# Another split of the rows over the partitions in a fused attention and mixer kernel: four rows of a head on 64 partitions, three on the other 64

## The chip, the cores and the metric

One core of a Trainium2 chip runs the whole program. The time is device microseconds (us) of one execution, as the median of several; lower is better. Ratios below are the mean time of one kernel's fast runs over that of the other's fast runs of the same rounds, so not quite the ratio of the medians that are quoted. A run counts as slow when it is over 1.5% above the fastest of its kernel.

## The reference, cut to what matters

Cosine attention over 8 batches, 12 heads, 448 rows and 64 columns a head, then a mixer with a token part and a channel part. Everything comes in and goes out as 32-bit floats.

```
q_n = q / (norm(q) + 1e-6);  k_n = k / (norm(k) + 1e-6)
attn = softmax(q_n @ k_n.T / tau)
x   = (attn @ v) as [8, 448, 768]
h   = relu(x.T @ w_tok1) @ w_tok2         # 448 -> 256 -> 448
u   = x + h.T
out = u + relu(u @ w_ch1) @ w_ch2         # 768 -> 1536 -> 768
```

## The kernel before

The difficulty is the 448 rows: three and a half times 128 partitions. The kernel keeps 384 rows of a head as three rows on each of 128 partitions (the main loads, pieces of 768 B) and the last 64 rows apart, as one row on each of 64 partitions (pieces of 256 B). Heads are taken in pairs (48 in all), pairs in half batches of three.

```
P, NC, XR = 128, 3, 64;  SM = P * NC                       # 384 main rows, 64 more
def main(at, src, nm, n, g0=0, g1=6, bufs=3):
    ...
    return dict(out=at[n][:, g0:g1].rearrange("p g c e -> p g (c e)"),
                in_=half(src, n)[g0:g1, 0:SM].rearrange("g (p c) e -> p g (c e)", c=NC))
def load_q(n, g0=0, g1=6):
    nc.sync.dma_start(**main(qm, q, "qm", n, g0, g1))        # k and v alike
def load_xq(b, g0=0, g1=12):
    ...
    nc.sync.dma_start(out=xq[b][:, g0:g1], in_=q[b, g0:g1, SM:S].rearrange("g p e -> p g e"))
def load_x2(...):                                            # xk, xv: two heads on two halves
    for g in range(2):
        eng.dma_start(out=at[b][XR * g:XR * (g + 1), g0 // 2:g1 // 2], in_=r[g])
def weights_tok():                                           # GpSimd issues
    nc.gpsimd.dma_start(out=w1t[:, 0:NC, :], ...)
    nc.gpsimd.dma_start(out=w1t[0:XR, NC, :], ...)
    nc.gpsimd.dma_start(out=w2n[0][:], ...)                  # the second token weight
def place_w2():                                              # three copies put it in order
    nc.vector.tensor_copy(out=w2t[:, :, XR:S]..., in_=w2n[0][:, :, 0:SM]...)
    for lo in (0, S):
        nc.vector.tensor_copy(out=w2t[:, :, lo:lo + XR], in_=w2n[0][:, :, SM:S])
...
# a store of an output row block
nc.sync.dma_start(out=out[b, 0:SM].rearrange("(p c) d -> c p d", c=NC)[m][:, cols], in_=o[:, cols])
```

Nearly all loads, all stores and the transposes by DMA (of u throughout, of q, k and x from pair 15 on) are issued by one engine, SyncE, in program order: "the queue" below. GpSimd issues the weights and scales and squares q and k; TensorE does all products.

Of the kernel before, what the change touches and what calls it, by code (L numbers as in the profile page):

```python
# [22 lines left out]
def kernel(  # L23
# [18 lines left out]

    P = 128
# [3 lines left out]
    E1 = E + 1  # L47
    DT = D // P
# [16 lines left out]
    qkv = ctx.enter_context(tc.tile_pool(name="qkv", bufs=3))  # L65
# [14 lines left out]
    sqx = cst.tile([P, 9, E], FP32, name="sqx")  # L80
    ssqs = [cst.tile([P, 45], FP32, name=f"ssq{i}") for i in range(3)]
    rns = [cst.tile([P, 45], FP32, name=f"rn{i}") for i in range(3)]
    kqs = [cst.tile([P, HP, 2, NC + 1, 2 * E], FP16, name=f"kq{i}") for i in range(2)]
    vts = [cst.tile([P, 6, NC, E + 2], FP16, name=f"vt{i}") for i in range(NV)]
    vxs = [cst.tile([P, HP, 2 * E1 + 2], FP16, name=f"vx{i}") for i in range(NV)]
# [3 lines left out]
    qm, km, vm, xq, xk, xv = {}, {}, {}, {}, {}, {}  # L89
# [4 lines left out]
    def half(src, n):  # L94
        return src[n // 2, 6 * (n % 2):6 * (n % 2) + 6]



    def main(at, src, nm, n, g0=0, g1=6, bufs=3):
        if n not in at:  # L100
            at[n] = qkv.tile([P, 6, NC, E], FP32, name=f"{nm}_{n}", tag=nm, bufs=bufs)
        return dict(out=at[n][:, g0:g1].rearrange("p g c e -> p g (c e)"),
                    in_=half(src, n)[g0:g1, 0:SM].rearrange("g (p c) e -> p g (c e)", c=NC))

    def load_q(n, g0=0, g1=6):
        nc.sync.dma_start(**main(qm, q, "qm", n, g0, g1))

    def load_k(n, g0=0, g1=6, eng=nc.sync):
        eng.dma_start(**main(km, k, "km", n, g0, g1))

    def load_v(n):
        nc.sync.dma_start(**main(vm, v, "vm", n, bufs=2))

    def load_xq(b, g0=0, g1=12):
        if b not in xq:
            xq[b] = qkv.tile([XR, H, E], FP32, name=f"xq_{b}", tag="xq", bufs=2)
        nc.sync.dma_start(out=xq[b][:, g0:g1], in_=q[b, g0:g1, SM:S].rearrange("g p e -> p g e"))

    def load_x2(at, src, nm, b, g0=0, g1=12, eng=nc.sync):
        if b not in at:  # L120
            at[b] = qkv.tile([P, NPAIR, E], FP32, name=f"{nm}_{b}", tag=nm, bufs=2)
        r = src[b, g0:g1, SM:S].rearrange("(j g) p e -> g p j e", g=2)
        for g in range(2):
            eng.dma_start(out=at[b][XR * g:XR * (g + 1), g0 // 2:g1 // 2], in_=r[g])  # L124

    def load_xk(b, g0=0, g1=12, eng=nc.sync):
        load_x2(xk, k, "xk", b, g0, g1, eng)

    def load_xv(b, g0=0, g1=12):
        load_x2(xv, v, "xv", b, g0, g1)  # L130



    def xh(at, n, w):
        return at[n // 2][:, w * (n % 2):w * (n % 2) + w]

    def mh(at, p):
        return at[p // HP][:, 2 * (p % HP):2 * (p % HP) + 2]

    def weights_tok():  # L140
        nc.gpsimd.dma_start(out=w1t[:, 0:NC, :], in_=moe_w_tok1[0:SM].rearrange("(p c) t -> p c t", c=NC))
        nc.gpsimd.dma_start(out=w1t[0:XR, NC, :], in_=moe_w_tok1[SM:S])
        w2n.append(mix.tile([P, TT, S], FP16, name="w2n", tag="gt16", bufs=1))
        nc.gpsimd.dma_start(out=w2n[0][:], in_=moe_w_tok2.rearrange("(tt p) s -> p tt s", p=P))

    def place_w2():
        nc.vector.tensor_copy(out=w2t[:, :, XR:S].rearrange("t a (c p) -> t a c p", c=NC),
                              in_=w2n[0][:, :, 0:SM].rearrange("t a (p c) -> t a c p", c=NC))
        for lo in (0, S):
            nc.vector.tensor_copy(out=w2t[:, :, lo:lo + XR], in_=w2n[0][:, :, SM:S])  # L150
# [12 lines left out]
    def cast_v(n):  # L163
        (nc.vector if n < 3 else nc.gpsimd).tensor_copy(out=vts[n % NV][:, :, :, 0:E].rearrange("p g c e -> p (g c) e"),
                              in_=vm[n][:].rearrange("p g c e -> p (g c) e"))
        for g in range(2):
            r = slice(XR * g, XR * (g + 1))
            nc.gpsimd.tensor_copy(out=vxs[n % NV][r, :, E1 * g:E1 * g + E], in_=xh(xv, n, HP)[r])

# [8 lines left out]
    def squares(p, eq, ek):  # L178
        sq[p] = nrm.tile([P, 2, 2 * NC, E], FP32, name=f"sq_{p}", tag="sq")
        for a, (eng, src) in enumerate(((eq, mh(qm, p)), (ek, mh(km, p)))):  # L180
            square(eng, sq[p][:, a], src.rearrange("p g c e -> p (g c) e"))

    def squares_x(n, eq, ek):
        square(eq, sqx[0:XR, 0:6], xh(xq, n, 6))
        square(ek, sqx[:, 6:9], xh(xk, n, HP))

    def sums(p, a0=0, a1=2):
        lo = 9 + 12 * (p % HP)
        nc.vector.tensor_reduce(out=ssqs[p // HP % 3][:, lo + 6 * a0:lo + 6 * a1],  # L189
                                in_=sq[p][:, a0:a1].rearrange("p a g e -> p (a g) e"), axis=AXX.X, op=ALU.add)  # L190

    def sums_x(n):
        nc.vector.tensor_reduce(out=ssqs[n % 3][:, 0:9], in_=sqx[:], axis=AXX.X, op=ALU.add)

    def rnorms(n, c0=0, c1=45):
        ssq, rn = ssqs[n % 3][:, c0:c1], rns[n % 3][:, c0:c1]
        nc.scalar.activation(out=rn, in_=ssq, func=AF.Ln, bias=tiny[:])
        nc.scalar.activation(out=rn, in_=rn, func=AF.Exp, scale=0.5)
        nc.scalar.activation(out=rn, in_=rn, func=AF.Ln, bias=eps[:])
        nc.scalar.activation(out=rn, in_=rn, func=AF.Exp, scale=-1.0)  # L200

    def scaled(p, eng):
        n, j = p // HP, p % HP
        for a, src in enumerate((mh(km, p), mh(qm, p))):
            lo = 9 + 12 * j + 6 * (1 - a)
            rn = rns[n % 3][:, lo:lo + 6].rearrange("p (g c) -> p g c", g=2)
            eng.tensor_tensor(out=kqs[n % 2][:, j, a, 0:NC, :].rearrange("p c (g e) -> p g c e", g=2),  # L207
                              in0=src, in1=_bcast_free(rn, E), op=ALU.mult)

    def scaled_x(n, eng, j0=0, j1=HP):  # L210
        rn, kq = rns[n % 3], kqs[n % 2]
        gs = slice(2 * j0, 2 * j1)
        eng.tensor_tensor(out=kq[0:XR, j0:j1, 1, NC, :].rearrange("p j (g e) -> p j g e", g=2),
                          in0=xh(xq, n, 6)[:, gs].rearrange("p (j g) e -> p j g e", g=2),
                          in1=_bcast_free(rn[0:XR, gs].rearrange("p (j g) -> p j g", g=2), E), op=ALU.mult)
        for g in range(2):
            r = slice(XR * g, XR * (g + 1))
            eng.tensor_tensor(out=kq[r, j0:j1, 0, NC, E * g:E * g + E], in0=xh(xk, n, HP)[r, j0:j1],
                              in1=_bcast_free(rn[r, 6 + j0:6 + j1], E), op=ALU.mult)
# [17 lines left out]
    def tpose_main(p, pst, a):  # L237
        for c in range(NC):
            nc.tensor.transpose(pst[:, P * (4 * a + c):P * (4 * a + c + 1)], kqs[p // HP % 2][:, p % HP, a, c], id16[:])  # L239

    def tpose_x(p, pst):
        kq = kqs[p // HP % 2]
        nc.tensor.transpose(pst[:, P * NC:P * (NC + 1)], kq[:, p % HP, 0, NC], id16[:])
        nc.tensor.transpose(pst[:, P * 7:P * 7 + XR], kq[0:XR, p % HP, 1, NC], id16[0:XR, 0:XR])
# [4 lines left out]
    def tpose(p):  # L249
        pst = pst_tile(p)  # L250
        tpose_main(p, pst, 0)
        tpose_main(p, pst, 1)
        tpose_x(p, pst)
# [11 lines left out]



    def score_main0(c, fill=0):
        qk, pt = qks[0], pts[0]
        psS = ps2.tile([P, 2, 512], FP32, name=f"psS_0_{c}", tag="s")  # L270
        busy(psS[:, 0, :], fill)
        for g in range(2):
            r = slice(E * g, E * g + E)
            nc.tensor.matmul(psS[:, g, 0:SM], qk[r, P * c:P * (c + 1)], qk[r, 512:512 + SM], start=True, stop=True)
        nc.scalar.activation(out=pt[:, 2 * S * c:2 * S * (c + 1)].rearrange("p (g s) -> p g s", g=2)[:, :, 0:SM],
                             in_=psS[:, :, 0:SM], func=AF.Exp, scale=inv_tau)

    def score_rest0():
        qk, pt = qks[0], pts[0]
        psS = ps2.tile([P, 2, 512], FP32, name="psS_0_r", tag="s")  # L280
        for c in range(NC):
            for g in range(2):
                r = slice(E * g, E * g + E)
                nc.tensor.matmul(psS[:, g, XR * c:XR * (c + 1)], qk[r, P * c:P * (c + 1)],
                                 qk[r, 512 + SM:512 + S], start=True, stop=True)
        for g in range(2):
# [191 lines left out]
    def loads(i):  # L478
        for n in q_at.get(i, ()):
            load_q(n)  # L480
        for b in xq_at.get(i, ()):
            load_xq(b)
# [277 lines left out]
```

## Time and profile before

| | before |
|---|---|
| time, median of the first three runs | 395.24 us (394.54 to 395.39) |
| span of the profiled execution | 395.6 us |
| TensorE busy | 379.0 us, 96% |
| loads and stores issued by the queue | 129, beside 108 transposes |
| queue occupied, 120 to 320 us | 162 of 200 us |

The queue is occupied for the sum of the durations of its rows in the timeline (small gaps between the issues of one row count in), in which the wait of an issue for its data is included. The lines of the page, the stretches and the waits stand in the prediction and are read there.

### The profile page before, as it was taken

How to read it: one execution, taken by the hardware profiler on the slowest of the kernel's cores; microseconds unless marked ns; L12 is line 12 of the kernel's file. 1: busy time of each engine (PE TensorE's matmuls, PEld its weight loads, DVE VectorE, ACT ScalarE, POOL GpSimd, SP SyncE). 2: the span in 40 equal slices, each digit the busy share in tenths (PEclk: the TensorE clock that was granted, in tenths of full speed). 3: DMA queues.
4: the chain of work that ended last, by engine and by line, in shares of the span. 5: the costliest groups of instructions: out<-in, count | busy, mean ns of one | idle time of the engine just before them, and what ended most of it. 6: DMA issues, size and time to landing. Idle time of an engine off the chain costs nothing.

```text
span 395.6 us, 9085 instructions
## 1 busy us (share of the span) xinstructions
PE 379.0 (96%) x3658; PEld 229.0 (58%) x3658; DVE 193.4 (49%) x368; ACT 226.3 (57%) x411; POOL 209.6 (53%) x306
## 2 busy tenths in 40 slices
PE   7498999998999999999999999999999999999997
PEld 2155656665556565656556666556556565666554
DVE  5668677964534555445623654536524442333022
ACT  5788799943485547675576347573676436510410
POOL 4957677579549393949492856749470800000000
PEclk9779999999999999999999999999999999999999
DMA  8999999989968988899999989999974363013013
GB/s 214 251 245 268 229 206 198 192 205 222 219 131 167 218 195 200 190 190 223 202 186 196 194 214 214 189 186 193 226 105 107 91 152 69 16 35 112 16 40 119
DMA packets 137482, 67.51 MB, mean 171 GB/s; under 512 B 93216, under 2 KB 133984, under 8 KB 137440
## 3 DMA queue, kind: packets, MB, share of 16 engines
q1 hardware_dynamic: 133264, 61.36, 72.1%
q0 software_dynamic: 3632, 5.18, 7.4%
q8 instruction: 28, 0.46, 0.5%
q10 hardware_dynamic: 544, 0.39, 0.3%
q14 instruction: 14, 0.11, 0.1%
HBM read 43.38 MB, written 11.01 MB: 138 GB/s over the span
## 4 chain that ended last, share of the span: by engine, by line
PE 87%; ACT 4%; DMA 4%; DVE 2%; SPq 1%; issue 0%; ACTq 0%; DVEq 0%
PE psF L400 28%; PE psG L385 27%; PE psO L316 9%; PE psS L297 7%; PE psR L337 5%; PE psU L357 4%; PE psO L318 3%; ACT pt L298 2%; PE psX L304 2%; DMA xk<-in_k_dram 2%; DMA km<-in_k_dram 1%; DMA out_dram<-ost 1%; PE psU L362 1%; PE pst L239 1%; DVE ost L403 1%; SPq L124 1%
## 5 line engine op out<-in xcount | busy, mean ns | idle before, releaser
L298 ACT ACTIVATE pt<-psS 128x896 f16<-128x896 f32 x141 | 119.0, 920 | 66.7 <-PE psS L297 66.5
L385 PE MATMUL psG<-ut,wc1t 128*128 128x448 f16 x576 | 119.5, 353 | 0.2
L400 PE MATMUL psF<-wc2t,gt 128*128 128x384 f16 (+2 forms) x684 | 117.3, 323 | 1.2 <-DVE ost L403 1.2
L387 ACT ACTIVATE gt<-psG 128x448 f16<-128x448 f32 x96 | 51.1, 556 | 73.2 <-PE psG L385 73.2
L400 PEld LDWEIGHTS <-gt 128*128 128x128 f16 x684 | 64.5, 98 | 48.4 <-issue 8.1
L207 POOL TENSOR_TENSOR kq<-km,rn 128x384 f16<-128x384 f32 x47 | 39.5, 841 | 85.0 <-ACT rn L200 84.7
L385 PEld LDWEIGHTS <-wc1t 128*128 128x128 f16 x576 | 53.2, 98 | 52.4 <-issue 8.7
L403 DVE TENSOR_TENSOR ost<-psF,ur 128x384 f32<-128x384 f32 (+2 forms) x57 | 31.4, 550 | 90.0 <-PE psF L400 86.6
L316 PEld LDWEIGHTS <-pt 128*128 128x128 f16 x1152 | 50.8, 98 | 11.3 <-issue 5.2
L316 PE MATMUL psO<-vt,pt 128*128 128x65 f16 x1152 | 53.2, 195 | 3.4 <-ACT pt L298 3.0
L322 DVE RECIPROCAL rec<-psO 128x8 f32<-128x8 f32 x48 | 9.9, 207 | 81.5 <-PE psO L318 81.4
L189 DVE TENSOR_REDUCE ssq<-sq 128x12 f32<-128x768 f32 (+1 forms) x49 | 45.1, 928 | 6.8 <-ACT sq L174 4.9
L318 PE MATMUL psO<-vx,pt 128*128 128x130 f16 x192 | 42.1, 219 | 0.0
L176 POOL TENSOR_TENSOR sq<-km 128x384 f32<-128x384 f32 x42 | 34.6, 826 | 11.3 <-DMA km<-in_k_dram 11.1
L207 POOL TENSOR_TENSOR kq<-qm,rn 128x384 f16<-128x384 f32 x47 | 39.6, 843 | 0.0
L297 PE MATMUL psS<-qk 64*128 64x448 f16 x282 | 36.5, 362 | 1.2 <-ACT pt L305 0.6
L323 DVE TENSOR_TENSOR x<-psO,rec 128x512 f16<-128x512 f32 x48 | 33.2, 691 | 1.7
L337 PE MATMUL psR<-x,w1t 128*128 128x128 f16 x384 | 29.2, 219 | 0.0
L305 ACT ACTIVATE pt<-psX 128x448 f16<-128x448 f32 x48 | 27.0, 563 | 3.5 <-PE psX L304 2.5
L357 PE MATMUL psU<-w2t,r 128*128 128x448 f16 x96 | 25.9, 353 | 1.8 <-DVE w2t L150 1.4
L176 POOL TENSOR_TENSOR sq<-qm 128x384 f32<-128x384 f32 x30 | 24.8, 827 | 3.7 <-DVE ssq L189 2.1
L337 PEld LDWEIGHTS <-w1t 128*128 128x128 f16 x384 | 23.8, 97 | 2.0 <-issue 0.3
(75 smaller groups left out, 319.8 us busy)
## 6 DMA issues: line engine op xcount, KB each, us to landing
vm<-in_v_dram SPq DMA_DIRECT2D x16, 576.0 KB, 5.4
out_dram<-ost SPq DMA_DIRECT2D x23, 384.0 KB, 3.1
qm<-in_q_dram SPq DMA_DIRECT2D x15, 576.0 KB, 5.4
km<-in_k_dram SPq DMA_DIRECT2D x15, 576.0 KB, 5.6
wc1t<-in_moe_w_ch_dram POOLq DMA_DIRECT2D x2, 1152.0 KB, 13.4
wc2t<-in_moe_w_ch_dram POOLq DMA_DIRECT2D x2, 1152.0 KB, 13.0
out_dram<-ost SPq DMA_DIRECT2D x9, 192.0 KB, 2.9
xq<-in_q_dram SPq DMA_DIRECT2D x7, 192.0 KB, 6.0
```

The lines of the kernel that those rows point to most:

```text
L176: eng.tensor_tensor(out=out, in0=src, in1=src, op=ALU.mult)
L189: nc.vector.tensor_reduce(out=ssqs[p // HP % 3][:, lo + 6 * a0:lo + 6 * a1], in_=sq[p][:, a0:a1].rearrange("p a g e -> p (a g) e"), axis=A ...
L207: eng.tensor_tensor(out=kqs[n % 2][:, j, a, 0:NC, :].rearrange("p c (g e) -> p g c e", g=2), in0=src, in1=_bcast_free(rn, E), op=ALU.mult)
L297: nc.tensor.matmul(psS[:, g, 0:S], qk[r, P * c:P * (c + 1)], qk[r, 512:512 + S], start=True, stop=True)
L298: nc.scalar.activation(out=pt[:, 2 * S * c:2 * S * (c + 1)].rearrange("p (g s) -> p g s", g=2), in_=psS[:, :, 0:S], func=AF.Exp, scale=inv ...
L316: nc.tensor.matmul(psO[:, m, E1 * g:E1 * (g + 1)], pt[:, at:at + P], vt[:, 2 * j + g, c, 0:E1], start=(g == 0 and c == 0), stop=False)
L318: nc.tensor.matmul(psO[:, m, 0:2 * E1], pt[:, PX + P * m:PX + P * (m + 1)], vx[:, j, 0:2 * E1], start=False, stop=True)
L337: nc.tensor.matmul(psR[:, tt, :], w1t[:, m, tt * P:(tt + 1) * P], xs[p][:, m, :], start=(m == 0), stop=(m == NC))
L357: nc.tensor.matmul(psU, rs[p][:, tt, :], w2t[:, tt, lo:lo + S], start=(tt == 0), stop=by_dma and tt == TT - 1)
L385: nc.tensor.matmul(psG[:], wc1t[:, dt, ct * P:(ct + 1) * P], ut[:, dt, sp], start=(dt == 0), stop=(dt == DT - 1))
L387: nc.scalar.activation(out=gt[:, ct, sp], in_=psG[:], func=AF.Relu)
L400: nc.tensor.matmul(psF[:, 0:w], gt[:, ct, lo:lo + P], wc2t[:, ct, P * i0:P * i1], start=(ct == 0), stop=(ct == CT - 1))
```

## The change

Its intent: drop the small loads. On 64 partitions a head has four rows, on the other 64 three (4 x 64 + 3 x 64 = 448), so the last 64 rows come with the main ones in pieces of 1024 or 768 B, and norms, scalings and casts lose their extra instructions for the last rows. For every second head of k and v the halves are mirrored, so that the fourth rows of two heads fill 128 partitions. No load of q, k or v spans 128 partitions. The second token weight is issued later, and slots 0 to 6 (one slot per pair) are ordered by hand.

```
+    def parts(mirrored):
+        four, three = (0, XR * CH, CH), (XR * CH, S, NC)        # CH = 4
+        if mirrored:
+            four, three = (XR * NC, S, CH), (0, XR * NC, NC)
+        return ((three, four) if mirrored else (four, three))
     def load_q(n, j0=0, j1=HP):
-        nc.sync.dma_start(**main(qm, q, "qm", n, g0, g1))
+        for i, (lo, hi, c) in enumerate(parts(False)):
+            nc.sync.dma_start(out=qms[n % 3][XR * i:XR * (i + 1), 2 * j0:2 * j1, 0:c]..., in_=...)
     def load_k(n, j0=0, j1=HP):                                  # v alike
+        for g in range(2):
+            for i in range(2):
+                load_heads(kms[n % 3], k, n, g, i, j0, j1)       # 64 partitions, 3 heads
-    load_xq, load_x2, load_xk, load_xv, squares_x, sums_x, scaled_x, score_main0, score_rest0
...
-            nc.sync.dma_start(out=out[b, 0:SM]...[m][:, cols], in_=o[:, cols])
+            for i, (r0, r1, c) in enumerate(parts(False)):
+                nc.sync.dma_start(out=out[b, r0:r1]...[m][:, cols], in_=o[XR * i:XR * (i + 1), cols])
...
     q_at: the load of q for half batch 7 (counted from 0) from slot 12 to slot 13
     weights_tok2() (the second token weight): from behind weights_tok1() to the end of slot 1
     place_w2(): four copies instead of three
... (slots 0 to 6 spelled out)
```

## The prediction

> **What bounds the kernel now.** I read the page first, then the busy time by stretches, then the waits of TensorE, then the chain of waits, then the order in time of each engine from 0 to 50 us and near 90 us.
>
> From the page, the engines' busy time and the 40 slices:
>
> ```profile
> PE 379.0 (96%) x3658; PEld 229.0 (58%) x3658; DVE 193.4 (49%) x368; ACT 226.3 (57%) x411; POOL 209.6 (53%) x306
> ...
> PE   7498999998999999999999999999999999999997
> ...
> PEclk9779999999999999999999999999999999999999
> ```
>
> TensorE is busy 379.0 of 395.6 us, so 16.6 us is all that any better order of the same matmuls can win, plus what a reduced clock costs. The stretches say where:
>
> ```profile
> 0.00:10.00 10.00, 7.37 (x28) 2.77 (x28) 5.34 (x15) 5.84 (x16) 4.74 (x21) 1.00 0.85 214
> 10.00:20.00 10.00, 4.25 (x37) 1.95 (x37) 6.12 (x11) 8.02 (x20) 9.15 (x14) 0.77 1.06 253
> 20.00:30.00 10.00, 8.84 (x97) 5.43 (x95) 7.22 (x12) 8.80 (x19) 5.66 (x7) 0.72 0.99 243
> 30.00:40.00 10.00, 8.59 (x130) 6.15 (x130) 7.83 (x16) 8.36 (x16) 7.50 (x12) 1.00 1.10 267
> ...
> 90.00:100.00 10.00, 8.83 (x88) 5.59 (x86) 4.52 (x10) 3.08 (x4) 9.71 (x15) 1.00 1.04 248
> ...
> 160.00:200.00 40.00, 40.00 (x389) 23.77 (x387) 20.85 (x43) 23.80 (x41) 29.32 (x42) 1.00 1.03 202
> ```
>
> Columns: stretch, length, busy TensorE, weight load, VectorE, ScalarE, GpSimd, granted clock, DMA share, GB/s. TensorE's gaps are 2.6, 5.8, 1.2 and 1.4 us in the first four stretches, 1.2 us at 90 to 100, none from 110 to 380, and about 2.9 us at the very end, where only the last store runs. The clock is 0.77 and 0.72 from 10 to 30 us. Everything winnable is thus in the first 100 us. The waits of TensorE name what ended the gaps:
>
> ```profile
> PE psO L316 <- ACT pt L298: 3.0, 2, 2.8
> PE pst L243 <- DVE kq L218: 1.8, 1, 1.8
> PE psU L357 <- DVE w2t L150: 1.4, 1, 1.4
> PE busy L232 <- POOL id L536: 1.4, 1, 1.4
> PE psF L400 <- DVE ost L403: 1.2, 1, 1.2
> ```
>
> And the chain of waits near the start shows a load behind the largest one:
>
> ```profile
> 11.51 6.98 DMA xk<-in_k_dram
> 18.49 0.03 ACTq L174
> 18.52 0.04 issue
> 18.56 0.36 ACT sqx L174
> 18.92 0.81 ACT pt L298
> ```
>
> The small load of the last 64 rows of k is under way for 6.98 us; ScalarE, which works in order, stands before its square until 18.56, and only then makes the exponentials of pair 1, on which the first output matmul (19.78) waits.
>
> [...] The removed loads move 256 B pieces. [...] with the queue full, the slices between 13.5 and 15.5 us move 106 to 206 GB/s, while the first main loads move about 340 to 375. [...] The trace has no half-partition main load; an issue takes 0.5 to 0.6 us on the queue whatever its size. [...] the granted clock is 0.50 from about 15.3 to 25.7 us, after a stretch (10 to 14 us) with 1.2 us of matmuls in 4.
>
> **The change part by part.**
>
> *Loads.* Removed: 96 heads x 64 rows x 3 tensors = 18,432 pieces of 256 B of 137,482 packets. Queue 1's 133,264 packets took 72.1% of 16 x 395.6 us, 34 ns each, so this takes away about 39 us of each DMA engine's 395: up to a tenth of the DMA load. From 110 us on TensorE never waits, so this counts only at the start. Added: half a batch took 3 main issues and on average 2.5 small ones; it now takes 10 (q 2, k 4, v 4). Each out row block becomes 2 stores. In all 96 more issues, at about 0.57 us, 55 us more of the queue's time.
>
> *Wider elementwise work.* Squares and scalings go from 384 to 512 columns. On GpSimd 192 to 384 columns is 503 to 827 ns, so 512 is about 1,043 ns. Per half: before, 6 scalings at 0.84 plus extra rows 0.84 + 2 x 0.525 = 6.95, squares 6.28, casts 1.18 + 0.69: 15.1 us. After: 12 x about 1.05 plus a cast of about 1.55: 14.2 us. VectorE sums: 3 x 0.945 + 0.744 = 3.58 before; 3 x (0.945 + 0.264) = 3.63 after. Neither is on the path after 110 us.
>
> *TensorE.* The same columns; 6 tiny matmuls of pair 0 go. Nothing.
>
> *The start, followed by hand with before's durations.* Pair 0 comes as six loads; the last is issued near 1.8 us, so k is squared near 5.0 (before 4.50). The k loads of pairs 1 and 2 are issued [...]near 4.1 to 5.8, and land near 9.5. ScalarE squares k of pair 1 before it copies the transposes of pair 0, so the first score moves from 10.18 to about 10.6. From there it is better: the whole score runs at once (no second part with its 1.8 and 0.9 us waits), the score of pair 1 comes near 15.3 (before 15.71), the exponentials of pair 1 no longer stand behind the late small load: they start near 16.5 instead of 18.83, the first output matmul near 17.4 to 18 instead of 19.78, the score of pair 2 near 21 instead of 23.88. So up to 2.8 us is won by then.
>
> *Then part is given back.* The load of the second token weight moves from 14.6 us to behind pair 5's squares on GpSimd. Its chain: scale pair 2 to 16.8, square pairs 3 and 4 to 18.9, norms of pair 3 done near 20, scale pair 3 to 22, square pair 5 to 23. Issued at 23, at some 5 us to landing (6.9 before, in a fuller queue), it lands near 28; VectorE then needs 2 us to place it: first product with it near 30.2, against 30.54. The gain shrinks from 2.8 to about 0.3 us. In slot 5 the new order puts norms (1.0 us) between the exponentials and the last one of pair 5, where before they stood a slot earlier beside an idle ScalarE: about 0.8 us given back. I make the start worth between -1 and +2 us, about +0.3.
>
> *Near 90 us.* The 1.2 us wait is for a store: it left at 92.43 although its data were ready near 85.3, because the queue stood before q's load (issued 89.33), which waited for GpSimd to release its buffer. The change moves this load one slot later, behind the stores. I count +1.2 us.
>
> *The end.* The last store becomes two issues of half the rows: about -0.4 us.
>
> Sum of the central terms: 0.3 + 1.2 - 0.4 = about 1.1 us off, so 394.1. The slots were evidently set by hand to fit, which my rough timing of the second weight may undervalue; I move to 393.5.
>
> **The rivals.**
>
> *The second weight decides.* For: TensorE already waited 1.4 us for its placement, and it is now issued some 8 us later. If it lands at 30, the start loses 1.5 us: about 396. If at 26, VectorE is ready near 27 anyway and 1.5 to 2 us are won: about 391.5.
>
> *The whole start is won.* If the pieces of 256 B were the real brake, loads land far earlier, [...]the clock stays full (worth up to 2.3 us) and nearly all of the 9 us of gaps from 8 to 50 us go: 386 to 388. Against: ScalarE is busy 8.0 to 8.8 of 10 us there; it becomes the bound first.
>
> *The issuing queue becomes the bound.* From 160 to 200 us it is occupied 36.9 of 40 us. About 7 us more would fill it, transposes would come late, and TensorE would wait in the steady part: 398 to 405. Against: much of the 36.9 us is the wait for GpSimd and VectorE inside an issue (a transpose takes 1.2 us at least and up to 3.6), and these results come no later than before.
>
> **Range and chances.** Two per cent is 7.9 us of a ceiling of roughly 12 (8 to 110 us) plus 2.3 of clock; only the second rival reaches it: 0.04. Slower by 2% needs the third in earnest: 0.03. Within 2%: 0.93. The range 390 to 397 spans the first rival's both ends with the 90 us term in or out.
>
> **What would show each step right or wrong.** Of the changed kernel: exponentials of pair 1 starting near 16.5; first output matmul before 18.5; half clock ending before 25.7; the wait for the placed weight still among TensorE's waits, with its first product near 30; the wait for ost near 97 gone; no waits of TensorE from 110 to 380; the end's gap longer by some 0.4 us; fewer packets under 512 B by 18,432. Waits of TensorE in the steady part for qk or xT would mean the queue; a first product with the placed weight before 28 us or score of pair 4 before 32 would mean that I undervalue the start.

## The result, and the profile after

| | before | after |
|---|---|---|
| time, median of 4 runs each | 395.31 us (394.54 to 396.47) | 427.47 us (425.51 to 429.47) |
| ratio | | 1.0811 (95%: 1.0754 to 1.0868) |
| span, mean granted clock | 395.6 us, 0.987 | 427.7 us, 0.961 |
| TensorE busy | 379.0 us | 388.8 us |
| loads and stores issued by the queue | 129 | 223 |
| queue occupied, 120 to 320 us | 162 us | 187 of 200 us |

The change made the kernel 8% slower. First the stretches of the kernel after, with the columns of the prediction's table:

```profile
10.00:20.00 10.00, 7.26 (x59) 3.61 (x57) 5.81 (x7) 7.26 (x16) 4.57 (x5) 0.79 1.08 223
20.00:30.00 10.00, 7.23 (x66) 4.40 (x64) 7.05 (x10) 7.28 (x16) 6.34 (x7) 0.53 1.12 223
30.00:40.00 10.00, 4.06 (x34) 2.49 (x34) 3.82 (x8) 2.54 (x3) 6.37 (x7) 0.82 1.15 225
...
90.00:100.00 10.00, 3.53 (x20) 2.04 (x20) 0.69 (x2) 1.29 (x4) 3.73 (x4) 0.72 1.24 175
...
200.00:320.00 120.00, 112.84 (x1087) 67.43 (x1085) 54.62 (x102) 64.41 (x111) 68.95 (x67) 0.99 0.86 184
```

and the one stretch of before that the prediction did not show:

```profile
200.00:320.00 120.00, 120.00 (x1182) 72.51 (x1181) 55.70 (x110) 70.66 (x120) 71.92 (x101) 1.00 0.88 178
```

The 32.1 us between the spans are 9.8 us of longer busy time (388.8 - 379.0, the same columns at a lower clock: see 0.53 from 20 to 30 and 0.72 from 90 to 100) and 22.3 us of idling. By stretch (rounded), idle time after minus before: 3.7 us from 0 to 50, 8.6 from 50 to 100, 1.2 from 100 to 200, 7.2 from 200 to 320 and 1.8 at the end (4.7 us behind the last product in place of 2.9). So TensorE loses in every part, and also where before it never waited. What it waited for, after:

```profile
PE psF L350 <- DMA wc2t<-in_moe_w_ch_dram: 7.3, 1, 7.3
PE psU L307 <- DVE w2t L144: 5.9, 1, 5.9
PE psG L335 <- DVE ost L353: 5.4, 3, 2.2
...
PE psS L208 <- DVE x L273: 2.7, 1, 2.7
PE psS L247 <- DVE ut L317: 2.0, 3, 1.1
```

Each line: the tile TensorE was to write, what released it, us in total, times, longest. Of the lines shown, the first is the landing of the second channel weight near 96 us, the second the placed second token weight at 37.2, the third output tiles that had not been stored yet, the last the sum that needs a transposed x from the queue. The second and fourth are of the start, the third and fifth of 110 to 330 us. The queue of the kernel after, in a stretch of that part (start, duration, issue):

```profile
203.61 1.62 SPq L236 DMA_TRANSPOSE qk<-kq  x1
205.32 1.68 SPq L280 DMA_TRANSPOSE xT<-x  x1
207.09 1.22 SPq L326 DMA_TRANSPOSE ur<-ut  x1
208.37 2.57 SPq L114 DMA_DIRECT2D km<-in_k_dram  x4
211.03 1.19 SPq L362 DMA_DIRECT2D out_dram<-ost  x2
212.33 1.36 SPq L236 DMA_TRANSPOSE qk<-kq  x1
```

and of the kernel before, for the same kind of slot:

```profile
189.89 0.57 SPq L112 DMA_DIRECT2D vm<-in_v_dram  x1
190.51 1.30 SPq L124 DMA_DIRECT2D xv<-in_v_dram  x2
191.91 0.56 SPq L410 DMA_DIRECT2D out_dram<-ost  x1
192.57 1.50 SPq L261 DMA_TRANSPOSE qk<-kq  x1
```

Each issue starts where the one before it ends. A load of k takes 2.57 us of the queue where a main load of 128 partitions (of v, above) took 0.57, and a store 1.19 instead of 0.56. The bytes are the same (67.5 MB in both), and the packets fell from 137,482 to 120,506.

### The profile page after: what moved, and what is told of

Its sections match the earlier page's. It is cut to its first block, busy times and chain, and to the rows that moved or that the text cites. A ratio compares the mean times of both kernels' runs of the same rounds, so it can differ in the third digit from the quotient of the medians.

```text
span 427.7 us, 9048 instructions
## 1 busy us (share of the span) xinstructions
PE 388.8 (91%) x3652; PEld 233.7 (55%) x3652; DVE 197.0 (46%) x354; ACT 224.7 (53%) x397; POOL 195.8 (46%) x204
## 2 busy tenths in 40 slices
DMA packets 120506, 67.51 MB, mean 158 GB/s; under 512 B 76304, under 2 KB 116944, under 8 KB 120464
## 4 chain that ended last, share of the span: by engine, by line
PE 63%; DMA 14%; SPq 8%; POOL 6%; DVE 3%; ACT 3%; issue 2%; DVEq 0%; POOLq 0%; ACTq 0%
PE psG L335 21%; PE psF L350 20%; PE psO L266 6%; SPq L114 5%; PE psS L247 5%; DMA wc2t<-in_moe_w_ch_dram 5%; POOL kq L194 4%; PE psR L287 3%; PE psU L307 3%; DMA km<-in_k_dram 3%; DMA out_dram<-ost 3%; DMA w2n<-in_moe_w_tok_dram 2%; DMA xT<-x 2%; PE psO L268 2%; POOL sq L172 2%
## 5 line engine op out<-in xcount | busy, mean ns | idle before, releaser
L248 ACT ACTIVATE pt<-psS 128x896 f16<-128x896 f32 x144 | 122.0, 920 | 72.2 <-PE psS L247 72.2
L194 POOL TENSOR_TENSOR kq<-km,rn 128x512 f16<-128x512 f32 x46 | 47.9, 1042 | 79.8 <-ACT rn L189 75.7
L172 POOL TENSOR_TENSOR sq<-km 128x512 f32<-128x512 f32 x42 | 43.8, 1046 | 40.8 <-DMA km<-in_k_dram 40.8
L180 DVE TENSOR_REDUCE ssq<-sq 128x16 f32<-128x1024 f32 (+1 forms) x49 | 57.9, 1188 | 8.4 <-POOL sq L172 4.4
L266 PEld LDWEIGHTS <-pt 128*128 128x128 f16 x1152 | 52.7, 100 | 6.9 <-issue 0.4
L266 PE MATMUL psO<-vt,pt 128*128 128x65 f16 x1152 | 55.4, 197 | 0.2
L194 POOL TENSOR_TENSOR kq<-qm,rn 128x512 f16<-128x512 f32 x46 | 50.7, 1102 | 0.0
L268 PE MATMUL psO<-vt,pt 128*128 128x130 f16 x192 | 43.1, 225 | 1.1 <-ACT pt L255 1.1
L172 POOL TENSOR_TENSOR sq<-qm 128x512 f32<-128x512 f32 x31 | 32.2, 1039 | 18.8 <-DMA qm<-in_q_dram 13.3
L247 PE MATMUL psS<-qk 64*128 64x448 f16 x288 | 37.7, 365 | 2.7 <-DVE ut L317 2.0
```

What stands on the lines that cost most here:

```text
L172: eng.tensor_tensor(out=out, in0=src, in1=src, op=ALU.mult)
L180: nc.vector.tensor_reduce(out=ssqs[p // HP % 3][:, p % HP, a0:a1].rearrange("p a g c -> p (a g c)"), in_=sq[p][:, a0:a1].rearrange("p a g ...
L194: eng.tensor_tensor(out=kqs[n % 2][:, j, a].rearrange("p c (g e) -> p g c e", g=2), in0=src, in1=_bcast_free(rns[n % 3][:, j, 1 - a], E), ...
L247: nc.tensor.matmul(psS[:, g, 0:S], qk[r, P * c:P * (c + 1)], qk[r, 512:512 + S], start=True, stop=True)
L248: nc.scalar.activation(out=pt[:, 2 * S * c:2 * S * (c + 1)].rearrange("p (g s) -> p g s", g=2), in_=psS[:, :, 0:S], func=AF.Exp, scale=inv ...
L266: nc.tensor.matmul(psO[:, m, E1 * g:E1 * (g + 1)], pt[:, at:at + P], vt[:, 2 * j + g, c, 0:E1], start=(g == 0 and c == 0), stop=False)
```

## The experiments

Eighteen kernels ran. They are ordered by question; "B" is the kernel before, "A" the kernel after.

### Loads over half of the partitions

**b_halves**, **b_heads**, **b_evenodd**: B, with each load of six heads (q, k and v) issued in two. All three have 46 loads more (175 in place of 129); they differ only in the cut.

```
+    for cut in (lambda t: t[0:XR],  lambda t: t[XR:P]):     # b_halves: lower and upper 64 partitions
+    for cut in (lambda t: t[:, 0:3], lambda t: t[:, 3:6]):   # b_heads: by heads, 128 partitions each
+    for cut in (lambda t: t[0:P:2], lambda t: t[1:P:2]):     # b_evenodd: even and odd partitions
         eng.dma_start(out=cut(a["out"]), in_=cut(a["in_"]))
```

> The kernel before, with each whole main load of q, k and v (6 heads, 128 partitions) cut into two loads of 64 partitions, lower and upper half; pieces, bytes and everything else stay. Theory 1 [...]: the plateaus of GB/s between 10 and 40 us fall to about 220, loads land later, and the time grows by a good part of the 32 us, say to 405 to 415. Theory 2 (the number of issues[...]): the same slowdown here and in the cut by heads. Theory 3 (the hand-set slots and the late second token weight are the cause, the loads are innocent): within 1% of before, 393 to 399.

> The kernel before, with each whole main load cut in two by heads: 128 partitions each, as many issues as in the cut by halves. Theory 1: within 1% of before (393 to 399), plateaus of 330 GB/s or more remain. Theory 2: as slow as the cut by halves.

> The kernel before, with each whole main load cut into the even and the odd partitions, 64 each. Theory 1: within 1% of before[...]; rates as in the cut by heads. Rival to it (any load of 64 partitions is slow[...]): as slow as the cut by halves.

Measured, beside B at 395.13: b_halves 404.97 (404.17 to 409.13; ratio 1.0257, 1.0193 to 1.0321), b_heads 397.25 (ratio 1.0035, 0.9992 to 1.0078), b_evenodd 396.07 (ratio 1.0005, 0.9962 to 1.0049). So 46 further issues cost about nothing, nor does a load of 64 partitions as such; a load of the lower or the upper 64 costs. What each moved from 10 to 20 us, in 40 slices of 0.25 us (GB/s), first b_halves:

```profile
GB/s 214 236 237 206 187 191 212 261 224 218 203 215 234 234 221 206 209 230 243 214 210 191 198 221 231 227 215 174 227 227 283 261 231 210 177 198 235 245 222 197
```

then b_evenodd:

```profile
GB/s 360 286 326 335 332 252 329 313 295 277 335 332 319 315 239 159 133 131 132 210 190 235 277 252 243 203 270 320 315 316 226 222 160 196 214 195 244 264 293 338
```

The halves stay at 174 to 283, 219 in the mean, with the DMA engines busy for 0.9 or more of every slice; the other cut moves 252 to 360 in its first 14 slices and 259 in the mean (B: 253). So the two cuts differ, 404.97 against 396.07 us; why they do was not shown.

**a_loads**: A, with the loads, stores and first token weight of B (128 partitions of three rows, small loads into the same tile); the slots of A kept.

```
-        for i, (lo, hi, c) in enumerate(parts(False)): ...
+        load_main(qms[n % 3], q, n); load_xq(n)                  # k, v: load_main and two small loads
```

> The changed kernel with the rows laid out and loaded as before (one main load of 128 partitions, the last 64 rows in pieces of 256 B), but into the merged tiles, with the merged elementwise work and the hand-set slots; stores as before. 8 load issues a half instead of 10. Theory 1: most of the 32 us come back, 392 to 402, and the second token weight lands less than 7 us after its issue. Theory 3: stays above 415.

Measured: 408.13 (406.81 to 409.8; ratio 1.0318). The transfers alone give back 19 of the 32 us, and no wait of TensorE is left between 120 and 320 us. A good part of the loss is elsewhere: TensorE still waits 6.0 us for the placed second token weight.

### The second token weight

**a_w2n**, **a_loads_w2n**: A and a_loads with the weight issued directly behind the first one, as in B. **b_w2n_late**: B with its issue moved behind slot 1's work on GpSimd.

```
         weights_tok1()
+        weights_tok2()          # a_w2n, a_loads_w2n; and taken out of slot 1
```

> The changed kernel with one line moved: the load of the second token weight is issued directly behind the first one (near 11 us) instead of behind pair 5's squares (26.6 us). Theory 1a (the half-partition loads cost about 20 us of the 32, the late weight about 6 of the rest): TensorE's wait of 5.9 us for the placed weight shrinks to below 2, and the time falls by 3 to 8 us, to 419 to 425. Rival (the weight only hides other lateness: POOL's norms and the loads behind it would be the next wait): within 2 us of 427.

> The changed kernel with before's row layout and loads (the run that took 408) and the second token weight issued early too. Theory 1a: another 4 to 9 us come back: 399 to 404. Rival: stays at 406 to 409, as the slots after it are set too late anyway.

> The kernel before with only the load of the second token weight moved behind all of slot 1's work on GpSimd. Theory 1a: it becomes TensorE's longest wait and costs 2 to 6 us: 397 to 401. Rival: nothing, 395 to 396.

Measured beside B at 394.96: a_w2n 428.21 (ratio 1.0834), a_loads_w2n 408.28 (1.0331), b_w2n_late 401.25 (401.05 to 401.38; 1.0159). The late issue does cost 6 us in B, where TensorE then waits 5.2 us, yet the early issue gains nothing in A. The theory that the landing was the one gate fell. VectorE's copies in a_loads_w2n show the second gate:

```profile
29.41 1.43 DVE L139 COPY w2t<-w2n 128x768 f16<-128x768 f16 x1
30.77 4.72 DVE L142 COPY w2t<-w2n 128x128 f16<-128x128 f16 x2
36.85 0.62 DVE L308 CAST ut<-psU 128x448 f16<-128x448 f32 x1 [1.37 <-PE psU L306]
```

Two copies of 128 columns take 4.72 us, where B's take 1.10 and a pair in A that starts behind GpSimd's block 0.35. They end at 35.49. GpSimd, meanwhile, in the same run:

```profile
29.39 1.04 POOL L188 TENSOR_TENSOR kq<-qm,rn 128x512 f16<-128x512 f32 x1
30.37 0.90 POOL L146 DMA_DIRECT2D wc1t<-in_moe_w_ch_dram  x1
31.29 1.06 POOL L188 TENSOR_TENSOR kq<-km,rn 128x512 f16<-128x512 f32 x1
32.29 1.05 POOL L188 TENSOR_TENSOR kq<-qm,rn 128x512 f16<-128x512 f32 x1
33.29 2.03 POOL L166 TENSOR_TENSOR sq<-km 128x512 f32<-128x512 f32 x2
```

It works without a gap until 35.32, just before the copies end. That alone is not enough: in B GpSimd also works without a gap of over 0.1 us, from 28.21 to 35.40, and the pair takes 1.10 in the middle of it; why VectorE gets in between there is not shown, nor what holds the copies in a_loads_w2n. Whether ScalarE's copies take as long beside such a block can be tried.

**a_loads_act**: a_loads_w2n with the same copies on ScalarE. **a_act** and **a_w2n_act**: the same edit to A and to a_w2n, which completes a table of two by two.

```
-        nc.vector.tensor_copy(out=w2t[...], in_=w2n[0][...])
+        nc.scalar.copy(out=w2t[...], in_=w2n[0][...])
```

> The changed kernel with the row layout and the loads of before and the second token weight issued early, as in the run before it of that kind (408.3 us), but the placement of that weight copied by ScalarE instead of VectorE. Theory (VectorE's small 16-bit copies starve while GpSimd works without a break from 28.4 to 35.3 us: 4.7 us for two copies of 128 columns): TensorE's 5.5 us wait for the placed weight falls below 1.5 us, the half clock between 30 and 40 us goes, the time falls to 399 to 403. Rival (something else ends at the same instant, the landing of the weight or a release): the wait stays near 5 us, 407 to 409.

> The changed kernel, only the placement of the second token weight copied by ScalarE; its load stays late (it landed at 35.08 us). Theory (in the changed kernel the landing is the gate, VectorE's starved copies only the second one behind it): no gain, and ScalarE, which works in order, now stands before its copies until the weight lands, so pair 3's exponentials come some 5 us later: 427 to 431. Rival (the copies were the only gate): 420 to 423.

> The changed kernel with both: the second token weight issued early and placed by ScalarE. Each alone gives nothing; theory (two gates in a row, each as long as the other): together they take TensorE's 5.9 us wait and the half clock after it away, 419 to 423. What then remains against the run with the loads of before and both of these (401.1) is what the half-partition loads and stores cost: 18 to 22 us, with DMA rates of 190 to 260 GB/s at the start, waits for the ch2 weight near 90 us and for store buffers between 180 and 330 us. Rival (the half-partition loads alone hold the start, whatever the second weight does): 426 to 429.

Measured: a_loads_act 401.11 (399.63 to 401.62; ratio 1.0141) beside B at 395.22, 7 us below a_loads_w2n. GpSimd has the same unbroken block (28.40 to 35.33), and ScalarE's copies beside it take 0.82 and, two together, 0.49 us:

```profile
28.65 0.82 ACT L139 COPY w2t<-w2n 128x768 f16<-128x768 f16 x1
29.39 0.49 ACT L142 COPY w2t<-w2n 128x128 f16<-128x128 f16 x2
```

The wait for the placed weight is gone, and the granted clock from 30 to 40 us is 1.00. On A itself:

| A's variants | copies by VectorE | copies by ScalarE |
|---|---|---|
| weight issued late | 427.47 | 428.39 (424.77 to 429.52) |
| weight issued early | 428.21 | 420.55 (419.98 to 424.35) |

Neither edit alone gains; both together gain 7 us. There are two gates that open at the same time: late, the weight lands at 35.08 us; early, VectorE's copies of 128 columns take 4.98 us and end at 37.9, GpSimd's block at 37.7. The expectation for a_w2n_act held.

### The four rows without the halves

**a_inter**: k and v as four rows on the even and three on the odd partitions (mirrored for the second head), q, the stores and the first weight as in B, the second weight issued early. It gave a **wrong result** (relative error 0.092): the clearing of the second v tile stood behind its load in program order and overwrote data. It ran at 423.44, with three of its four runs, the profiled one among them, slow; nothing is concluded from it. **a_inter2** moves that clearing ahead and copies the weight by ScalarE.

> The changed kernel with its four-and-three layout for k and v put on even and odd partitions instead of lower and upper half ([...]no 256 B pieces for k and v), q loaded as before, stores as before, the second token weight early. Theory 1: the DMA runs at 300 GB/s or more in the first 30 us and the time is at least as good as that of the run with before's loads and the early weight: 395 to 403. Rival (64-partition loads or their number cost by themselves): slower than that run by 5 us or more.

> The earlier run with k and v loaded as four rows on the even and three on the odd partitions, with its fault mended (the clearing of the second v tile stands ahead of the loads), and the weight placed by ScalarE. It must be correct now. Theory (the halves of the partitions, not the four-and-three rows, cost the time): DMA rate above 300 GB/s in the full slices, and a time within 3 us of the run with the loads of before and ScalarE's copies, 398 to 405. Rival (the four-and-three layout or the number of issues costs by itself): over 410.

Measured for a_inter2: correct, 409.27 (406.17 to 412.5; the 412.5 is slow, the three fast runs have a mean of 408.2, ratio 1.0328). The theory missed: with no halves in its k and v loads, it is still 7 us slower than a_loads_act. 3.9 us are a wait for the second channel weight, 1.8 us are my own clearing by DMA. It has 200 loads and stores on the queue in place of a_loads_act's 162. I read it as a hint that the number of issues counts after all, against b_heads and b_evenodd.

### The number of transfers

**b_stores**: B with each store of 128 partitions cut into lower and upper 64, loads unchanged.

> The kernel before with each store of 128 partitions cut into a lower and an upper half of the partitions, loads unchanged. Theory ([...]the queue has 24 to 32 issues more): the gap after the last product grows from 2.9 to about 4.3 us and some waits of TensorE for the store buffer come between 180 and 330 us, 2 to 5 us in all: 396.5 to 400. Rival (only the loads matter): within 1 us of 395.

Measured: 397.69 (397.33 to 398.14; ratio 1.0065). TensorE has no new wait before the end; behind its last product come 5.0 us instead of 2.9. So the stores alone cost 2.5 us, 2.1 of them at the end of the kernel, and make no wait in the middle.

**b_quarters**: B with A's pattern of transfers: q in two, k and v in four (two halves of the partitions by two head parities), stores in two. **b_quarters_eo**: the same numbers, cut into even and odd partitions.

```
+        for g in range(heads):                              # heads = 2 for k and v, 1 for q
+            for lo, hi in ((0, XR), (XR, P)):               # b_quarters_eo: 0:P:2 and 1:P:2
+                eng.dma_start(out=a["out"][lo:hi, g::heads], in_=a["in_"][lo:hi, g::heads])
```

> The kernel before with the changed kernel's pattern of transfers: each whole load of q in two halves of the partitions, of k and v in two halves by the heads' parity (four loads each), each store in two halves; data layout and slots of before. What the changed kernel loses by its transfers is 19.4 us by the runs so far (420.6 against 401.1); q, k, v halves alone cost 10, stores alone 2.6. Theory (halves and their number together make the 19 us): 409 to 417. Rival (the rest lies in something else of the changed layout): 404 to 408.

> The same numbers of loads and stores of 64 partitions and the same bytes, but even and odd partitions in place of the lower and the upper 64. Theory (it is the halves, not the number of issues): 395 to 399. Rival (the number of issues on the one queue): within 3 us of the run beside it.

Measured beside B at 395.57: b_quarters 425.6 (424.53 to 426.72; ratio 1.0752, 1.072 to 1.0784), b_quarters_eo 421.62 (420.94 to 424.73; 1.0675, 1.0632 to 1.0717). My theory of halves missed by 23 us here: with every whole load and store cut over even and odd partitions, and nothing else of A's, the kernel loses 26 us. (With 263 loads and stores it has 40 more than A, because B's small loads stay.) The halves add 4. DMA bandwidth is not what b_quarters_eo lacks: from 120 to 320 us its DMA engines are busy for 0.78 of the time, B's for 0.90. Its rates from 10 to 20 us:

```profile
GB/s 120 124 45 83 89 126 338 356 353 363 366 338 277 191 212 289 320 298 295 126 25 52 61 129 152 149 203 209 200 185 166 169 157 156 185 174 194 193 257 318
```

At 15 us they fall to 25, with the DMA engines some 40 to 60% busy, while the queue is issuing one load after the other:

```profile
10.69 2.59 SPq L108 DMA_DIRECT2D km<-in_k_dram  x4
13.32 0.61 SPq L122 DMA_DIRECT2D xq<-in_q_dram  x1
13.98 1.28 SPq L129 DMA_DIRECT2D xk<-in_k_dram  x2
```

In B, the same small loads of k were issued from 10.24 on. Later, from 110 to 330 us, where B has no wait at all, TensorE waits in b_quarters_eo:

```profile
PE psG L390 <- DVE ost L408: 5.6, 2, 2.9
PE psS L302 <- DVE ut L372: 4.6, 7, 0.9
PE psS L302 <- DMA qk<-kq: 4.3, 5, 2.4
```

These are the output tiles not yet stored and the transposes that came late: all products of the one queue. Waits for earlier transfers are not it either: between 120 and 320 us no issue of this queue waits for the landing of an earlier transfer, in B, A or b_quarters_eo; in the whole of b_quarters_eo such waits sum to 6.3 us (in A to 17.4, 16.5 of them before 120 us). In order of the loads and stores on that queue, the runs stand so (those named a_ have A's slots besides, so it is no pure series):

| kernel | loads and stores on the queue | queue occupied, 120 to 320 us | time |
|---|---|---|---|
| B | 129 | 162 | 395.3 |
| b_stores (halves) | 155 | 170 | 397.7 |
| a_loads_act | 162 | 176 | 401.1 |
| b_heads | 175 | 168 | 397.3 |
| b_evenodd | 175 | 174 | 396.1 |
| b_halves (halves) | 175 | 176 | 405.0 |
| a_inter2 | 200 | 181 | 408.2 (mean of the fast runs) |
| a_w2n_act (halves) | 223 | 187 | 420.6 |
| A (halves) | 223 | 187 | 427.5 |
| b_quarters_eo | 263 | 190 | 421.6 |
| b_quarters (halves) | 263 | 189 | 425.6 |

The third column is in us, of 200. In b_heads and b_evenodd the queue's slack takes 46 issues more (within 2.2 us); near 187 of 200 it has next to none. The slack itself, the gaps of over 0.15 us between one issue's end and the next one's start, sums over these 200 us to 27.4 us in B, 22.1 in b_heads, 14.8 in b_evenodd, 3.6 in A and 0.8 in b_quarters_eo.

### The terms that the prediction called winnable

**b_q7**: B with q's load for half batch 7 one slot later, as A has it. **b_best1**: with it, the two small copies of the second weight by ScalarE and the cast of the second v batch behind them. **b_best2**: with that, the squares of the last 64 rows of the second half batch behind pair 1's exponentials.

```
-    q_at = ... 10 if n == 6 else 3 * n - 9
+    q_at = ... {6: 10, 7: 13}.get(n, 3 * n - 9)                       # b_q7
+            nc.scalar.copy(out=w2t[:, :, lo:lo + XR], ...)            # b_best1; and cast_v(1) behind place_w2()
+            if i == 1: squares_x(1, nc.scalar, nc.scalar)              # b_best2: behind score(1, ...)
```

> The kernel before with the load of q for the seventh half batch moved one slot later, as the change does it. The prediction's term near 90 us: the 1.2 us wait for the store buffer near 97 us goes, nothing else moves: 393.9 to 394.4 against 395.1. Rival (it only shifts the wait to another product): within 0.3 us of before.

> The kernel before with q's seventh load one slot later (394.0 alone), the two small copies of the second weight's placement on ScalarE and the cast of the second v batch behind the placement. Theory: the 1.4 us wait for the placed weight at 30 us goes too: 392.4 to 393.6, about 0.5% faster than before. Rival (ScalarE is the bound there and only moves its exponentials): 393.7 to 394.6.

> The same, and the squares of the last 64 rows of the second half batch moved behind the exponentials of pair 1 on ScalarE, so that these no longer stand behind the small load that lands at 18.5 us. The prediction's chain: exponentials of pair 1 at 17.6 instead of 18.83, first output matmul near 18.6 instead of 19.78, worth up to 1.2 us and a shorter half clock: 391 to 393. Rival (the norms of pair 3 come later instead and a later wait eats it): equal to the run beside it.

Measured: b_q7 393.99 (393.38 to 394.44; ratio 0.9967, 0.9952 to 0.9982) beside B at 395.22; in the rounds of b_best1 and b_best2 B stood at 395.63, b_best1 at 393.49 (392.26 to 394.36; ratio 0.9936, 0.9907 to 0.9965) and b_best2 at 394.91 (0.9969). In b_q7 the wait for the store buffer near 97 us is gone. In b_best1 the wait for the placed weight is 0.4 us instead of 1.4. In b_best2 the exponentials of pair 1 start at 16.88 instead of 18.83 and the first output product at 17.85 instead of 19.78, but 2.1 us come back as a wait at 22.30 for the copied transposes of the next pair: the rival of that run was right, and the chain near the start is one of several of the same length. b_best1 is the fastest kernel here: 0.6% below B, its interval clear of 1, and 8% below A.

## Why the prediction was wrong

It said 393.5 us, with 390 to 397 as the range and 0.03 for slower by 2%; 427.47 came. Point by point:

- **Loads: the step that failed first.** The prediction put it so: "In all 96 more issues, at about 0.57 us, 55 us more of the queue's time." The count was right (94 measured on this queue). It then gave these 55 us no price in its sum. In its place the runs showed that these issues fill the queue (162 to 187 of 200 us) and that transposes and stores behind them come late: b_quarters_eo, with added issues (134) and nothing else of the change, costs 26 us.
- **The third rival, "the issuing queue becomes the bound"**, was therefore the right one, and was argued away: much of the queue's time "is the wait for GpSimd and VectorE inside an issue", and these results come no later. This reading does not come out of B's trace: of the 36.9 us from 160 to 200, 17 transposes take 24.8 and 14 loads and stores 9.6. At the shortest seen there (1.22 and 0.56 us) they would take 28.5, so, as an estimate, at most about 6 us are waits (the transposes there take up to 2.2 us; the one of 3.6 starts at 200.0). Nor was a wait on the queue filled by a later issue: in B a store whose data were written by 85.27 us left at 92.43, behind q's load, before which the queue stood from 81.54 to 89.33. So added issues come on top once the gaps between issues (27.4 us from 120 to 320 in B, 3.6 in A) are used up. In A TensorE idles for 7.6 us from 120 to 320 us, which is within the rival's 398 to 405; the rest of A's loss lies elsewhere. For the issues of b_quarters_eo that size was too small: there TensorE idles for 14.6 us from 120 to 320 us, its first output product comes 2.6 us later (22.34 against 19.78), and at a lower mean granted clock (0.975 against 0.987) its busy time is 6.4 us longer (385.4 against 379.0).
- **The halves.** The prediction found no load over half of the partitions in B's trace and gave such loads no number. Between b_halves and b_evenodd, which have the same count, it is 9 us; at b_quarters' count 4 us.
- **The second weight.** The first rival had it at 30 at worst: about 396. It was issued at 26.64 in place of 23 (k's load landed late, at 19.97) and took 8.42 us in place of 5: 35.08. The wait of TensorE was 5.9 us, and the granted clock was 0.50 from about 36.3 to 43.2 us. Beyond that, a second gate that the prediction did not see, VectorE's copies beside GpSimd's unbroken block, would have held it anyway. Together they are worth 7 us (427.5 against 420.6).
- **The early part of the start was right in direction, too large in size.** Exponentials of pair 1 from 16.98 (predicted 16.5), the first output product at 18.83 (17.4 to 18, and to be before 18.5; 19.78 before). Half clock was to end before 25.7; it did not: it lasted to about 29.5, with 0.53 in the mean from 20 to 30 us.
- **Near 90 us.** The sign and the size were right (b_q7: 1.2 us), but in A this gain drowned: the queue was late there, and the second channel weight, issued at 69.0 and 76.4 us instead of 59.6 and 63.7, brought a wait of 7.3 us.
- **The end.** Predicted 0.4 us; 1.8 measured in A, and 2.1 in b_stores, for each halved store takes two issues of about 0.6 us and the queue's last stores follow each other.
- **Packets.** The 256 B pieces fell by exactly the 18,432 predicted (87,552 to 69,120). Packets under 512 B fell by 16,912 (93,216 to 76,304), because 95 more transfers brought 1,520 packets of 4 B, 16 each. Whether these pieces held B back was not tried apart; taking them away did not make up for the issues. (The slices that the prediction quotes from 13.5 to 15.5 us reach 227 GB/s, not 206.)
- **The wider elementwise work was sized right:** GpSimd's 512 columns take 1,042 to 1,102 ns on average (predicted 1,043 to 1,050), VectorE's sums 1,209 (945 + 264).

Taken apart by the runs, A's 32.2 us are: 7 for the second weight and its placement (A to a_w2n_act), 19.4 for the transfers (a_w2n_act to a_loads_act), and 5.8 for what is left in a_loads_act against B. That the cutting of the transfers costs more than the halves is shown on B at 263 loads and stores (26 and 4 of 30 us); at 175 it is the other way round (about 1 and 9 us); on A itself the two were not separated. That the number acts through the issue time of the one queue is read from the traces (the used-up gaps, the late transposes and stores) and not tested: no run gave the added issues to another engine, or added as many issues without making the transfers smaller. **Open** stays what the 5.8 us are: a_loads_act has 33 issues more than B and the slots by hand, and the two were not tried apart. Open too: the shares of loads and stores within the number. The late channel weight near 90 us takes both the transfers and the slots by hand: with A's slots and B's transfers the wait is 1.5 us (a_loads) or 1.0 (a_loads_act) in place of 7.3, and b_quarters and b_quarters_eo, with B's slots, do not have it.

## What to carry to other kernels

Count the issues on a queue that carries loads, stores and transposes in order, and compare their sum with the time that the queue has left: here a third more loads and stores cost nothing measurable, and twice as many 26 us. If rows have to be split over the partitions, split them so that each transfer spans all of them or every second one, not the lower or upper half: with 46 loads more the time here was 1.0035, 1.0005 and 1.0257 of B's. When a wait does not move although its first cause is taken away, look for a second gate that opens at the same time before dropping the theory.
